# A fused attention and gated-FFN kernel: its front put in another order

## The chip, the core and the metric

The kernel runs on one core of one Trainium2 chip, with one launch. Times are device microseconds of that core; a span is the time from the first to the last instruction of a profiled execution.

## The reference, cut to what matters

```
x: 2048 x 512 float32;  32 heads of 16;  F = 1792
q = x @ wq (32 heads);  k = x @ wk, v = x @ wv (16 wide, one for all heads)
a = softmax(q k^T / 4) v, heads side by side, @ wo
b = ((x @ w_gate) * (x @ w_up)) @ w_down
g = sigmoid(sum(x * gate_w))
out = g * a + (1 - g) * b
```

## The kernel before, in words

**Precision.** Each projection splits both operands into a high part (fp32r) and the rest, low part, and adds three products: high by high, low by high, high by low (`mm3`, `proj`). So a projection of a block of 512 rows of x with 128 output columns is four chunks of 128 inputs times three products: twelve matmuls of 128 by 512.

**Blocks and units.** x is handled in four blocks of 512 rows (c = 0 to 3). Each is transposed on TensorE (`x_trans0` for block 0, tile by tile; `x_trans` for the others, chunk by chunk) and split: `split` makes the high part on ScalarE and the low part on VectorE, both out of PSUM; chunks in `pool` are copied twice by ScalarE and the low part is made by GpSimd. `split2` makes both parts of something that lies in SBUF on GpSimd. K and V of a block come from one projection (`kv`), whose evacuation makes K (called KK, on ScalarE and then VectorE), and `v_trans` turns V. K's and V's weights are split by `kv_split`, the gate's by `gate_split`.

Q is projected in groups of 128 columns (g = 0 to 3, eight heads each), stored to DRAM as two tensors (`dq`, high and low) and fetched back by unit (`q_fetch`, six DMAs a unit): a unit is one tile of 128 query rows of one group. There are 64 units.

**Two passes over the scores.** For each unit, pass one (`p1`) computes scores with queries on the partitions, a matmul of 48 rows by 512 keys, and VectorE takes each row's maximum (L717). When the 32 maxima of a unit are there, `p1_end` reduces them and sends them through DRAM into two rows of the unit's Q tile. Pass two (`p2`) computes the scores transposed, with the maximum subtracted by those rows, and ScalarE takes the exponent (L758). `pv` multiplies by V, two key tiles at a time, eight matmuls in four column groups, and after 16 key tiles the accumulator is evacuated. The score matmuls use half of TensorE's rows (partitions 0 to 63 or 64 to 127), so two can run beside each other; so do the matmuls of the jobs below (L885).

**Jobs.** The rest of the work, projections of Q, the FFN's gate, up and down products and the output projection, is cut into jobs of 12 products, each issued in two halves of 64 rows, one half of the array each, the second half one job behind the first. Jobs fill the places between the scores.

**What sets the order.** Instructions are issued in program order on each engine. Until the lead loop the order is written out by hand (L779 to L811). The lead loop (L953) then interleaves pass one with `LEADJOBS` jobs until 25 steps of pass one (50 maxima) are done. The main loop goes through a written pattern (`ORDER`, `APART`) of pass one, pass two, job halves and PV; model times decide only which job is ready. When it ends, the jobs left over are issued, and then the last unit's output: sums and picks out of the accumulator (L673), a last output projection in two halves of columns (L150, 128 by 256), and the final stores.

**The front, L779 to L811.** Fourteen transposes of the identity; block 0 of x; K/V of block 0; Q of group 0 from block 0, stored whole; the fetch of units 0 and 1; loads of the other Q weights; transposes of blocks 1 and 2; K/V of block 1; then K/V of blocks 2 and 3 and block 3's transposes with five steps of pass one (`steps`) between them. Block 3's first two chunks have their low part made by GpSimd. The loads of x (`load_x`) are all issued at the start on SyncE's queue (SP), but for block 0's last tile and the small weights, which ScalarE issues. A load waits on SP until the one eight places earlier has landed.

Of the kernel before, what the change touches and what calls it, by code (L numbers as in the profile page):

```python
# [26 lines left out]
NG = 4  # L27
NT = 4
# [17 lines left out]
PV_IN, PV_ROUND, PV_LAST, PV_END, PV_OUT = 331.0, 866.0, 438.0, 617.0, 647.0  # L46
NB = 7
LAT, LAT_LAST = 1.0, 0.5
LEADJOBS = 6
O0, O1 = 0, 0  # L50


# [17 lines left out]
def mix_kernel(ctx: ExitStack, tc: tile.TileContext, x, wq, wk, wv, wo, wg, wu, wd, gw, out):  # L70
# [86 lines left out]
    def bank(i, name):  # L157
        return psum.tile([128, 512], F32, name=name, tag=f"bank{i}")
# [4 lines left out]
    def load_x(c):  # L163
        if c < 2:
            xn = [w512("y", F32, 8) for _ in range(NT)]
        else:
            pairs = [work.tile([128, 2, 512], F32, name="P", tag="P", bufs=PBUF) for _ in range(2)]
            xn = [t[:, i] for t in pairs for i in range(2)]
        for t in range(NT):
            eng = nc.scalar if c == 0 and t == NT - 1 else nc.sync  # L170
            eng.dma_start(xn[t], x2[c * 512 + t * 128:c * 512 + t * 128 + 128, :])
        return xn

    def stage(src, tag="wn", bufs=4):
        n = w512(tag, F32, bufs)
        nc.sync.dma_start(n.rearrange("p (k f) -> p k f", k=4) if len(src.shape) == 3 else n, src)
        return n
# [21 lines left out]
                nc.sync.dma_start(xT[c][v][k].bitcast(F32), xd[c][v * 4 + k])  # L199

    dq, dqat = {}, {}

    def at(t, fn):
        later(max(0.0, t - clock["T"]), fn)
# [13 lines left out]
    def q_fetch(u):  # L218
        c, g, t = units[u]
        q = Q[u] = work.tile([128, 4, 128], F32R, name="Q", tag="Q", bufs=QB)  # L220
        for d, rows in zip(dq[c, g], ((0, 32), (16,))):
            for half in range(2):
                for r in rows:
                    b = half * 64 + r
                    src = d[half * 64:half * 64 + 64, t * 128:(t + 1) * 128]
                    nc.sync.dma_start(q[b:b + 16].bitcast(F32), src.rearrange("(s d) q -> d s q", d=DH))
        qat[u] = clock["T"] + 6000.0

    kvn = work.tile([128, 4, 32], F32, name="kvn", tag="oT", bufs=2)
    nc.scalar.dma_start(kvn[:, :, 0:16], wk_v)  # L230
    nc.scalar.dma_start(kvn[:, :, 16:32], wv_v)
    gwn = work.tile([128, 128], F32, name="gwn", tag="rb", bufs=2)
    nc.scalar.dma_start(gwn[0:4], gw.rearrange("(k p) -> k p", p=128))
    xns = {0: load_x(0)}
    wqn = [stage(wq_v[:, :, 0:128])]
    xns[1] = load_x(1)
    xns[2] = load_x(2)
    xns[3] = load_x(3)
# [6 lines left out]
    def kv_split():  # L245
        nc.vector.tensor_copy(kvs2[0], kvn)
# [7 lines left out]
        split2(*wqs[0], wqn[0])  # L254

    def gate_split():

        p = bank(6, "warm")
        nc.tensor.transpose(p[:, 0:4], gwn[0:4], ident[0:4, 0:4])
        hi, lo = (wkvt[:, v].rearrange("p (k c) -> p k c", k=4)[:, :, 58] for v in range(2))  # L260
        split(hi, lo, p[:, 0:4])

    def x_trans0():
        xT[0] = x_tiles()
        hi, lo = xT[0][2:]
        for t in range(NT):
            p = bank(2 + t, "px")
            for k in range(4):
                nc.tensor.transpose(p[:, KS[k]], xns[0][t][:, KS[k]], ident)  # L269
            split(hi[:, :, KS[t]], lo[:, :, KS[t]], p.rearrange("p (k q) -> p k q", k=4))  # L270
            if t == 1:
                kv_split()
                gate_split()

    def x_trans(c, ks=range(4), pool=()):
        xn = xns[c]
        if c not in xT:
            xT[c] = [[w[:, k] for k in range(4)] for w in (woh, wol)] if c == 3 else \
                x_tiles((("hh", "hl"), ("wdh", "wdl"))[c - 1])
        for k in ks:  # L280
            p = bank(2 + (4 * c + k) % 5, "px")
            for t in range(NT):
                nc.tensor.transpose(p[:, KS[t]], xn[t][:, KS[k]], ident)  # L283
            if k in pool:
                xs = w512(("yt", "osb")[k % 2], F32, 2)
                nc.scalar.copy(xT[c][0][k], p)
                nc.scalar.copy(xs, p)
                nc.gpsimd.tensor_tensor(xT[c][1][k], xs, xT[c][0][k].bitcast(F32), op=OP.subtract)
            else:
                split(xT[c][0][k], xT[c][1][k], p)  # L290

    kvs = {}

    def kv(c, between=None):
        p = ms_bank(c % 2)
# [9 lines left out]
        nc.scalar.activation(Kc, p, AF.Identity, bias=kneg)  # L305
        nc.vector.scalar_tensor_tensor(Kc, Kc.bitcast(F32), klow, p, op0=OP.mult, op1=OP.add)  # L306
        nc.scalar.copy(kvs[c], p)

    def v_trans(c):
        pv = bank(7, "pv")  # L310
# [19 lines left out]
    def q_evac(c, g, p, fast=False):  # L330
        qh, ql = w512("oh", F32R, 2), w512("ol", F32R, 2)
        if fast:
            split(qh, ql, p)
# [219 lines left out]

    def ffn_jobs():
        for c in range(NC):
            yield from q_jobs(c, range(c == 0, NG))
        pend = None
        for i, (c, f) in enumerate(order):
            if f == 0:
                hat = {}  # L560
            gu, wdn = {}, []
            yield ffn_job(i, 0, gu, hat, wdn)
            wdn.append(stage(wd[f * 128:(f + 1) * 128, :], "wdn", 2))
            if st["idle"]:
                later(4000.0, lambda wdn=wdn: wd_split(wdn))
            yield ffn_job(i, 1, gu, hat, wdn)
            if f == NF - 1:
                ends = [pend, down_jobs(c, FGS[-1], hat)]
                for k in LAST:
                    yield next(ends[k])  # L570
                pend = None
            elif pend and f != NF - 2:
                yield from pend
                pend = None
            for fs in FGS[:-1]:
                if f == fs[-1]:
                    pend = down_jobs(c, fs, hat)
# [198 lines left out]
            later(0.0, out)  # L776


    p = bank(6, "warm")  # L779
    for i in range(14):  # L780
        nc.tensor.transpose(p[:, KS[i % 4]], ident, ident)  # L781
    x_trans0()
    kv(0)
    p = ms_bank(1)
    mm_all(p, proj(wqs[0], xT[0]))
    q_evac(0, 0, p, True)
    for u in range(2):
        q_fetch(u)
    for g in range(1, NG):
        wqn.append(stage(wq_v[:, :, g * 128:(g + 1) * 128]))  # L790
    x_trans(1)
    x_trans(2)
    kv(1)
    v_trans(0)
    x_trans(3, (0, 1), (0, 1))
    done = 0

    def steps(n, banks):
        nonlocal done
        for i in range(2 * n):  # L800
            p1(done + i // 2, i % 2, banks[i])
        done += n

    steps(1, (3, 7))
    x_trans(3, (2, 3))
    kv(2, lambda: steps(1, (4, 5)))
    steps(1, (6, 2))
    for g in range(1, NG):
        split2(*wqs[g], wqn[g])
    v_trans(1)  # L810
# [204 lines left out]
```

## Time and profile before

| | us |
|---|---|
| median of 3 runs (lowest, highest) | 1617.45 (1617.38, 1618.65) |
| span of the profiled execution | 1616.4 |
| TensorE busy in it | 1608.8 |
| VectorE busy | 1382.5 |
| ScalarE busy | 1227.2 |
| GpSimd busy | 732.9 |
| mean granted TensorE clock | 0.999 |

For the profiled execution the trace gives the span alone, without what lies around it; the runs of the same kernel are 1.0 to 2.2 us longer than that span.

How to read the rows below. A row of the timeline has start, duration, engine, line of the kernel, operation, output and inputs, shape, how many equal instructions follow each other, and in brackets the engine's idle time ahead of it and what ended that. A row of windows has the stretch and its length, then the busy time (and instructions) of PE, the weight loads, DVE, ACT and POOL, the granted clock, the DMA engines' share and GB/s. A row of groups has the count, busy time in us, mean ns of one, and the idle time ahead of them. PE is TensorE, PEld its weight loads, DVE VectorE, ACT ScalarE, POOL GpSimd, SPq SyncE's queue. Matmuls overlap, so one that takes 0.39 us can follow its neighbour by 0.23.

### The profile page before, as it was taken

The numbers are of one execution on the slowest core, as the hardware profiler recorded it, in microseconds if no ns is written. First come the engines' busy times: TensorE is split into PE (matmuls) and PEld (weight loads), VectorE is DVE, ScalarE is ACT, GpSimd is POOL, SyncE is SP. The second block draws the span as 40 slices with busy tenths as digits, with TensorE's granted clock in tenths as the row PEclk, the third lists the DMA queues.
The fourth block names the chain that finished last, engine by engine and source line by source line (L and its number), as shares of the span: only waits on it lengthen the run. The fifth ranks groups of instructions, "written<-read, shape, count | busy, mean of one in ns | idle before, by whom it ended". The sixth has DMA issues, their size and how long they took to land.

```text
span 1616.4 us, 35356 instructions
## 1 busy us (share of the span) xinstructions
PE 1608.8 (100%) x13139; PEld 1029.4 (64%) x13139; DVE 1382.5 (86%) x2412; ACT 1227.2 (76%) x2368; POOL 732.9 (45%) x869
## 2 busy tenths in 40 slices
PE   9999999999999999999999999999999999999998
PEld 7766666666666666666666666666666666666564
DVE  6988888888888888888888888888888888888870
ACT  4477777777778777777788787787788787787786
POOL 3325652634644542535543651642643642643633
PEclk9999999999999999999999999999999999999999
DMA  4463321212322221212231221222231221221111
GB/s 155 147 238 114 95 71 54 65 54 69 94 68 71 67 74 52 66 48 72 64 102 59 74 66 53 67 59 61 66 112 48 72 79 49 65 66 56 41 30 40
DMA packets 185255, 121.45 MB, mean 75 GB/s; under 512 B 46328, under 2 KB 154748, under 8 KB 185084
## 3 DMA queue, kind: packets, MB, share of 16 engines
q1 hardware_dynamic: 183732, 118.74, 24.3%
q8 instruction: 103, 1.69, 0.4%
q10 hardware_dynamic: 1352, 0.46, 0.1%
q14 instruction: 68, 0.56, 0.1%
HBM read 82.96 MB, written 36.17 MB: 74 GB/s over the span
## 4 chain that ended last, share of the span: by engine, by line
PE 99%; ACT 1%; DVE 0%; issue 0%; POOL 0%; DVEq 0%; POOLq 0%; ACTq 0%
PE ms L885 34%; PE acc L770 29%; PE s L757 18%; PE s L716 15%; PE ms L150 1%; ACT P L758 1%; PE px L283 0%; PE warm L781 0%; PE wo L150 0%; ACT yt L354 0%; PE pv L312 0%; ACT osb L774 0%; PE px L269 0%; POOL P L251 0%; DVE KK L306 0%
## 5 line engine op out<-in xcount | busy, mean ns | idle before, releaser
L717 DVE TENSOR_REDUCE mx<-s 128x1 f32<-128x512 f32 x2048 | 1308.8, 685 | 168.9 <-PE s L716 82.6
L758 ACT ACTIVATE P<-s 128x512 f32<-128x512 f32 x2048 | 1079.3, 606 | 260.1 <-PE s L757 221.4
L757 PE MATMUL s<-Q,KK 50*128 50x512 f32 x2048 | 746.0, 411 | 0.1
L716 PE MATMUL s<-KK,Q 48*128 48x512 f32 x2048 | 691.5, 406 | 0.7 <-ACT gb L315 0.5
L770 PE MATMUL acc<-P,V 128*32 128x512 f32 x4096 | 493.5, 598 | 0.0
L757 PEld LDWEIGHTS s<-Q,KK 50*128 50x128 f32 x2048 | 352.2, 185 | 177.7 <-issue 94.7
L716 PEld LDWEIGHTS s<-KK,Q 48*128 48x128 f32 x2048 | 337.9, 185 | 109.2 <-ACT P L758 48.5
L885 PE MATMUL ms<-xh,wh 64*128 64x512 f32 x920 | 338.4, 391 | 0.0
L885 PE MATMUL ms<-xl,wh 64*128 64x512 f32 x920 | 337.3, 391 | 0.0
L885 PE MATMUL ms<-xh,wl 64*128 64x512 f32 x920 | 321.5, 391 | 0.0
L770 PEld LDWEIGHTS acc<-P,V 128*32 128x32 f32 x4096 | 108.5, 109 | 236.3 <-issue 196.1
L528 POOL TENSOR_TENSOR hf<-gs 128x512 f32<-128x512 f32 x56 | 71.9, 1284 | 355.9 <-ACT gs L519 340.6
L355 POOL TENSOR_TENSOR y<-y,yt 128x512 f32<-128x512 f32 x79 | 101.3, 1286 | 230.4 <-ACT yt L354 223.4
L885 PEld LDWEIGHTS ms<-xl,wh 64*128 64x128 f32 x920 | 164.5, 186 | 10.2
L885 PEld LDWEIGHTS ms<-xh,wh 64*128 64x128 f32 x920 | 163.5, 186 | 10.3 <-POOL wl L138 0.4
L885 PE MATMUL ms<-wdh,hh 64*128 64x512 f32 x448 | 165.0, 393 | 0.0
L885 PE MATMUL ms<-wdl,hh 64*128 64x512 f32 x448 | 165.0, 391 | 0.0
L885 PEld LDWEIGHTS ms<-xh,wl 64*128 64x128 f32 x920 | 157.1, 186 | 10.1 <-issue 0.3
L885 PE MATMUL ms<-wdh,hl 64*128 64x512 f32 x448 | 158.7, 391 | 0.0
L138 POOL TENSOR_TENSOR wl<-wn,wh 128x512 fp32r<-128x512 f32 x117 | 150.5, 1287 | 9.4
L774 ACT COPY osb<-acc 128x512 f32<-128x512 f32 x64 | 37.5, 586 | 76.0 <-PE acc L770 76.0
L629 POOL TENSOR_TENSOR oT<-raw,rb 128x128 f32<-128x128 f32 x63 | 29.0, 461 | 126.0 <-DMA rb<-dr 126.0
(156 smaller groups left out, 1314.4 us busy)
## 6 DMA issues: line engine op xcount, KB each, us to landing
do<-osb SPq DMA_DIRECT2D x63, 256.0 KB
wn<-in_B_w_gate_dram SPq DMA_DIRECT2D x56, 256.0 KB
wn<-in_B_w_up_dram SPq DMA_DIRECT2D x56, 256.0 KB
wdn<-in_B_w_down_dram SPq DMA_DIRECT2D x56, 256.0 KB
Q<-dq SPq DMA_DIRECT2D x384, 32.0 KB
raw<-do SPq DMA_DIRECT2D x252, 32.0 KB
dq<-oh SPq DMA_DIRECT2D x16, 256.0 KB
dq<-ol SPq DMA_DIRECT2D x16, 256.0 KB
```

The lines of the kernel that those rows point to most:

```text
L138: nc.gpsimd.tensor_tensor(lo, src, hi.bitcast(F32), op=OP.subtract)
L150: nc.tensor.matmul(p, l, r, start=start and i == 0, stop=stop and i == len(prods) - 1)
L355: nc.gpsimd.tensor_tensor(y[c, t], y[c, t], tmp, op=OP.add)
L528: nc.gpsimd.tensor_tensor(hf, gu[0], gu[1], op=OP.mult)
L629: nc.gpsimd.tensor_tensor(dst, raw[:, 0], rb, op=OP.mult)
L716: nc.tensor.matmul(p, q[r, slot], KK[r, kq * 512:(kq + 1) * 512], start=True, stop=True)
L717: nc.vector.tensor_reduce(mx[u][:, half * 4 + slot, kq:kq + 1], p, axis=AX.X, op=OP.max)
L757: nc.tensor.matmul(p, KK[r, j * 128:(j + 1) * 128], q[r].rearrange("p s q -> p (s q)"), start=True, stop=True)
L758: nc.scalar.activation(P[s][:, half], p, AF.Exp, scale=0.25)
L770: nc.tensor.matmul(acc[u][b:b + 32, :], V[:, j + i], src[:, half], start=(j == 0), stop=(j == NJ - 2))
L774: nc.scalar.copy(osb, acc.pop(u))
L885: nc.tensor.matmul(p, lhs[HALVES[l]], rhs[HALVES[l]], start=(i == 0 and (l == 0 or j.apart)), stop=(end and (l == 1 or j.apart)))
```

## The change

The order of the front is written anew. Block 0's four x tiles are loaded two on SP and two on ScalarE's queue, ahead of everything else, with wq's first group behind them; K/V's weights come later, and block 3 of x is loaded behind the first fetch of Q. Three more identity transposes stand behind each of block 0's last three tiles. Q of group 0 is projected first, in two halves of 256 columns with stores of their own (`q_first`), and unit 0 is fetched after the first half is stored; K/V's weights are split behind that. Blocks 2 and 3 of x have all their low parts made by GpSimd out of ScalarE's copies. Twelve steps of pass one, not five, stand in the front, in groups of two steps (four matmuls) between the K/V blocks. Q of group 1 from block 0 is projected in the front as well (at full height, twelve matmuls), and the lead loop takes four jobs instead of six: with Q of group 1 that makes five early jobs.

```diff
-LEADJOBS = 6
+LEADJOBS = 4
@@ load_x
-            eng = nc.scalar if c == 0 and t == NT - 1 else nc.sync
+            eng = nc.scalar if c == 0 and t % 2 else nc.sync
@@ q_fetch
-        for d, rows in zip(dq[c, g], ((0, 32), (16,))):
+        parts = dq[c, g]
+        if len(parts) > 2:
+            parts, t = parts[t // 2 * 2:t // 2 * 2 + 2], t % 2
+        for d, rows in zip(parts, ((0, 32), (16,))):
@@ loads
+    xns = {0: load_x(0)}
+    wqn = [stage(wq_v[:, :, 0:128])]
     kvn = work.tile([128, 4, 32], F32, name="kvn", tag="oT", bufs=2)
...
-    xns = {0: load_x(0)}
-    wqn = [stage(wq_v[:, :, 0:128])]
     xns[1] = load_x(1)
     xns[2] = load_x(2)
-    xns[3] = load_x(3)
@@ x_trans0
-            if t == 1:
-                kv_split()
-                gate_split()
+            if t:
+                warm(3)
-    def x_trans(c, ks=range(4), pool=()):
+    def x_trans(c, ks=range(4), banks=(), pool=()):
...
-        for k in ks:
-            p = bank(2 + (4 * c + k) % 5, "px")
+        for k, b in zip(ks, banks):
+            p = bank(b, "px")
@@
+    def q_first():
+        qh, ql = w512("oh", F32R, 2), w512("ol", F32R, 2)
+        dq[0, 0], stores = [], []
+        for i, cols in enumerate(HALF):
+            p = ms_bank(i)[:, 0:256]
+            mm_all(p, [(l, r[:, cols]) for l, r in proj(wqs[0], xT[0])])
+            split(qh[:, cols], ql[:, cols], p)
+            for src in (qh, ql):
+                d = dram.tile([128, 256], F32, name=f"dq{len(stores)}", bufs=1)
+                dq[0, 0].append(d)
+                stores.append(lambda d=d, src=src, cols=cols: nc.sync.dma_start(d, src[:, cols].bitcast(F32)))
+        dqat[0, 0] = 0.0
+        return stores
+
+    def q_evac(c, g, p, now=False):
+        qh, ql = w512("oh", F32R, 2), w512("ol", F32R, 2)
+        if now:
+            qs = w512("gs", F32, 3)
+            nc.scalar.copy(qs, p)
+            split2(qh, ql, qs)
             q_store(c, g, qh, ql)
@@ ffn_jobs
-            yield from q_jobs(c, range(c == 0, NG))
+            yield from q_jobs(c, range(2 * (c == 0), NG))
@@ the front
-    kv(0)
-    p = ms_bank(1)
-    mm_all(p, proj(wqs[0], xT[0]))
-    q_evac(0, 0, p, True)
-    for u in range(2):
-        q_fetch(u)
+    split2(*wqs[0], wqn[0])
+    stores = q_first()
+    kv_split()
+    gate_split()
+    for f in stores[:2]:
+        f()
+    q_fetch(0)
+    x_trans(1, banks=(2, 3, 4, 5))
+    kv(0, 0)
+    x_trans(2, banks=(1, 2, 3, 4), pool=range(4))
+    xns[3] = load_x(3)
     for g in range(1, NG):
         wqn.append(stage(wq_v[:, :, g * 128:(g + 1) * 128]))
-    x_trans(1)
-    x_trans(2)
-    kv(1)
-    v_trans(0)
-    x_trans(3, (0, 1), (0, 1))
+    for f in stores[2:]:
+        f()
+    q_fetch(1)
...
-            p1(done + i // 2, i % 2, banks[i])
+            p1(done + i // 2, i % 2, (5, 6, 7, 0)[(2 * done + i) % 4])
...
-    steps(1, (3, 7))
-    x_trans(3, (2, 3))
-    kv(2, lambda: steps(1, (4, 5)))
-    steps(1, (6, 2))
-    for g in range(1, NG):
+    steps(2)
+    kv(1, 1, lambda: steps(2))
+    split2(*wqs[1], wqn[1])
+    v_trans(0, 2)
+    x_trans(3, (0, 1), (3, 4), range(4))
+    steps(2)
+    x_trans(3, (2, 3), (1, 2), range(4))
+    steps(2)
+    kv(2, 3)
+    q1 = proj(wqs[1], xT[0])
+    p = ms_bank(4)
+    mm_all(p, q1[:6], True, False)
+    steps(2)
+    mm_all(p, q1[6:], False, True)
+    q_evac(0, 1, p, True)
+    st["q"] += 1
+    for g in range(2, NG):
         split2(*wqs[g], wqn[g])
-    v_trans(1)
-    kv(3, lambda: steps(2, (3,4,5,6)))
+    v_trans(1, 2)
+    kv(3, 1, lambda: steps(2))
```

More of the change, by code (lines that the diff above doesn't have):

```diff
@@ L201, in mix_kernel @@
     dq, dqat = {}, {}
+    HALF = (slice(0, 256), slice(256, 512))
     def at(t, fn):
@@ L253, in kv_split @@
             eng.tensor_copy(w[:, :, :, 50:58], kvs2[v][:, :, 16:32].rearrange("p k (h d) -> p k h d", h=2))
-        split2(*wqs[0], wqn[0])
     def gate_split():
@@ L292, in mix_kernel, with kv @@
     kvs = {}
-    def kv(c, between=None):
-        p = ms_bank(c % 2)
+    def kv(c, b, between=None):
+        p = ms_bank(b)
         prods = proj((wkvh, wkvl), xT[c])
@@ L307, in kv, with v_trans @@
         nc.scalar.copy(kvs[c], p)
-    def v_trans(c):
-        pv = bank(7, "pv")
+    def v_trans(c, b=7):
+        pv = bank(b, "pv")
         for t in range(4):
@@ L328, in gates @@
         nc.vector.tensor_scalar(gb, gg, -1.0, 1.0, op0=OP.mult, op1=OP.add)
-    def q_evac(c, g, p, fast=False):
+    def q_first():
         qh, ql = w512("oh", F32R, 2), w512("ol", F32R, 2)
-        if fast:
-            split(qh, ql, p)
+        dq[0, 0], stores = [], []
[15 more added lines that the diff above has]
+            split2(qh, ql, qs)
             q_store(c, g, qh, ql)
@@ L776, in pv, with warm, steps @@
             later(0.0, out)
-    p = bank(6, "warm")
-    for i in range(14):
-        nc.tensor.transpose(p[:, KS[i % 4]], ident, ident)
-    x_trans0()
-    kv(0)
-    p = ms_bank(1)
-    mm_all(p, proj(wqs[0], xT[0]))
-    q_evac(0, 0, p, True)
-    for u in range(2):
-        q_fetch(u)
+    wp = bank(6, "warm")
+    def warm(n):
+        for i in range(n):
+            nc.tensor.transpose(wp[:, KS[i % 4]], ident, ident)
+    warm(14)
+    x_trans0()
+    split2(*wqs[0], wqn[0])
[9 more added lines that the diff above has]
+    xns[3] = load_x(3)
     for g in range(1, NG):
         wqn.append(stage(wq_v[:, :, g * 128:(g + 1) * 128]))
-    x_trans(1)
-    x_trans(2)
-    kv(1)
-    v_trans(0)
-    x_trans(3, (0, 1), (0, 1))
+    for f in stores[2:]:
+        f()
+    q_fetch(1)
     done = 0
-    def steps(n, banks):
+    def steps(n):
         nonlocal done
         for i in range(2 * n):
-            p1(done + i // 2, i % 2, banks[i])
+            p1(done + i // 2, i % 2, (5, 6, 7, 0)[(2 * done + i) % 4])
         done += n
-    steps(1, (3, 7))
-    x_trans(3, (2, 3))
-    kv(2, lambda: steps(1, (4, 5)))
-    steps(1, (6, 2))
-    for g in range(1, NG):
+    steps(2)
[15 more added lines that the diff above has]
+    for g in range(2, NG):
         split2(*wqs[g], wqn[g])
-    v_trans(1)
-    kv(3, lambda: steps(2, (3,4,5,6)))
+    v_trans(1, 2)
+    kv(3, 1, lambda: steps(2))
     xT_first = dict(xT)
```

## The prediction

> **What bounds the kernel now.** I read the page first: busy time per engine and the chain that ended last.
>
> ```profile
> PE 1608.8 (100%) x13139; PEld 1029.4 (64%) x13139; DVE 1382.5 (86%) x2412; ACT 1227.2 (76%) x2368; POOL 732.9 (45%) x869
> PE 99%; ACT 1%; DVE 0%; issue 0%; POOL 0%; DVEq 0%; POOLq 0%; ACTq 0%
> ```
>
> TensorE (PE) holds 99% of the chain, so the sum of its work is fixed and an edit can only remove or add time in which it waits, at the two ends. The instruction order says the same: from the first to the last score in the main loop both programs issue the same kinds of matmul in the same order, only that every job sits one place later. So I read the timeline of the front, and then of the end.
>
> ```profile
> 24.58 0.69 DVE L717 TENSOR_REDUCE mx<-s 128x1 f32<-128x512 f32 x1
> L717 DVE TENSOR_REDUCE mx<-s 128x1 f32<-128x512 f32 x49 | 30.1, 680 | 1.3 <-PE s L716 1.1
> 34.55:60.50 25.95, 25.95 (x180) 20.73 (x180) 24.99 (x47) 3.96 (x8) 7.60 (x8) 1.00 0.21 74
> 60.50 0.50 PE L757 MATMUL s<-Q,KK 50*128 50x512 f32 x1
> 71.24 1.92 PE L770 MATMUL acc<-P,V 128*32 128x512 f32 x16
> ```
>
> The first maximum is reduced at 24.58 us, the first exponent score is issued at 60.50, the first PV at 71.24. The second row groups VectorE (DVE) from 24 to 61 us: 49 maxima, 30.1 us (0.614 each), with only 1.3 us of waiting ahead of them. The third (span, then PE, weight loads, DVE) has DVE at 24.99 of 25.95 us. So **DVE bounds the front from the first maximum to the first exponent score**: 50 maxima lie between them, before and after the change alike.
>
> **The change, part by part.**
>
> *First Q projection ahead of K/V.* On PE, the opening of the program, before (ms is a projection's bank, xh/xl the transposed x, P the K/V weights, wh/wl the Q weights):
>
> ```order
> L269 MATMUL px<-ident,y 128x128 x8
> L150 MATMUL ms_200<-xh,P 128x512 x8
> L150 MATMUL ms_200<-xl,P 128x512 x4
> L150 MATMUL ms_217<-xh,wh 128x512
> L283 MATMUL px<-ident,y 128x128 x16
> L283 MATMUL px<-ident,P 128x128 x16
> L150 MATMUL ms_330<-hh,P 128x512 x2
> ```
>
> And after, from the end of the Q projection to the first maxima (s):
>
> ```order
> L150 MATMUL ms_210<-xl,wh 128x256
> L261 MATMUL warm<-ident,gwn 128x4
> L284 MATMUL px<-ident,y 128x128 x16
> L150 MATMUL ms_284<-xh,P 128x512 x8
> L150 MATMUL ms_284<-xl,P 128x512 x4
> L284 MATMUL px<-ident,P 128x128 x16
> L733 MATMUL s_367<-KK,Q 128x512
> L733 MATMUL s_376<-KK,Q 128x512
> L150 MATMUL ms_379<-hh,P 128x512 x2
> ```
>
> Q (ms_193 and ms_210, two halves of 256 columns) now precedes K/V (ms_284), and the first maxima stand ahead of the second K/V block instead of behind it and a third set of transposes.
>
> ```profile
> 7.50 0.66 PE L269 MATMUL px<-ident,y 128*128 128x128 f32 x4 [0.70 <-DMA y<-in_A_x_dram]
> 8.82 0.61 POOL L137 CAST wh<-wn 128x512 fp32r<-128x512 f32 x1
> 9.52 1.27 POOL L138 TENSOR_TENSOR wl<-wn,wh 128x512 fp32r<-128x512 f32 x1
> 1610.06 0.28 PE L150 MATMUL wo<-woh,ol 128*128 128x256 f32 x1
> 1610.17 0.28 PE L150 MATMUL wo<-wol,oh 128*128 128x256 f32 x1
> 16.05 1.91 PE L283 MATMUL px<-ident,y 128*128 128x128 f32 x16
> 16.86 0.33 SPq L210 DMA_DIRECT2D dq<-oh  x1
> 18.94 5.95 SPq L226 DMA_DIRECT2D Q<-dq  x12
> 6.08 4.43 SPq L171 DMA_DIRECT2D P<-in_A_x_dram  x8
> ```
>
> The last x tile came at 7.50 us; in the new order of loads the weights follow close behind it, so I put wn at 6.7. GpSimd (POOL) then needs 0.61 + 1.27 us: wl at 8.65. 24 half-width matmuls at 0.115 (two neighbours in the tail) end at 11.4, against 16.05. Half 0 is evacuated and stored from 10.8; a store took 2.08 us to let the fetch go (16.86 to 18.94), a fetch 0.5 us to issue (5.95/12), so the six for unit 0 are out by 15.8 and land, with another 2, by 17.8. SP has x2's loads ahead of the store; x2's and x3's were all issued by 10.5 before, and x3's four now follow the fetch.
>
> K/V of block 0 must wait for its weights, which DVE now splits behind Q's evacuation (ends 12.6).
>
> ```profile
> 7.32 0.22 DVE L246 CAST rb<-kvn 128x128 fp32r<-128x128 f32 x1
> 8.37 0.15 DVE L143 TENSOR_TENSOR P<-warm,P 128x4 fp32r<-128x4 f32 x1
> 15.14 0.39 PE L150 MATMUL ms<-xl,wh 128*128 128x512 f32 x1
> 15.37 0.39 PE L150 MATMUL ms<-xh,wh 128*128 128x512 f32 x1
> 22.85 0.69 ACT L305 ACTIVATE KK<-ms,kneg 128x512 fp32r<-128x512 f32 x1 [2.10 <-PE ms L150]
> 23.57 0.75 DVE L306 SCALAR_TENSOR_TENSOR KK<-KK,klow,ms 128x512 fp32r<-128x512 f32 x1 [1.23 <-ACT KK L305]
> ```
>
> The split ran from 7.32 to 8.52, so it is done at 13.8 (block 1's transposes cover it on PE); twelve matmuls 0.23 apart end at 16.5; ScalarE (ACT) and DVE make K by 0.69 + 0.75: 18.3. Sixteen transposes (1.91) fill PE until 18.5. **First maxima matmul 18.5, first reduce 19.05: 5.5 us earlier.** Q has 0.7 us to spare there.
>
> *Chunks split on ACT and POOL.* The low halves of x2 and of x3's second half leave DVE.
>
> ```profile
> L143 DVE TENSOR_TENSOR wol<-px,woh 128x512 fp32r<-128x512 f32 x2 | 1.3, 685 | 1.2 <-ACT woh L142 1.2
> 25.36 0.62 ACT L287 COPY yt<-px 128x512 f32<-128x512 f32 x1
> 25.84 0.63 ACT L286 CAST woh<-px 128x512 fp32r<-128x512 f32 x1
> 26.06 1.29 POOL L288 TENSOR_TENSOR wol<-yt,woh 128x512 fp32r<-128x512 f32 x1 [15.27 <-ACT yt L287]
> ```
>
> Inside the bound stretch that frees 1.3 us of DVE (x2's four lay ahead of it). In return ACT makes two passes per chunk, 0.48 apart, eight for a block: 18.9 to 22.8 for x2, which lets the second K/V block start only at 20.0 (its bank is a transpose's). POOL's eight halves at 1.29 and the split of wq1 (0.61 + 1.27) run from 20 to 32.3, each ahead of its reader.
>
> *Maxima woven in.* Four maxima matmuls use four banks and the next four wait for their reduces, while PE, in order, keeps whole K/V blocks between them. Stepping through the order with the durations above, DVE stands idle at 21.5 (0.4, bank), 25.4 (0.4, K block 1), 30.7 to 32.4 and 33.2 to 33.7 (2.2: sixteen maxima are used up and K block 2, twelve matmuls behind the sixteenth, must come first), 36.3 (1.3, second half of Q 1), 40.9 (0.8, K block 3 and wl of Q 2) and some 0.3 more: 5.3 us, against 1.3 before. PE enters the lead loop at 39.0 instead of 34.55, but with 24 maxima done instead of 10.
>
> Each such group changes PE's tile shape twice.
>
> ```profile
> 32.00 0.40 PE L150 MATMUL ms<-wol,P 128*128 128x512 f32 x1
> 32.33 0.30 PEld L716 LDWEIGHTS s<-KK,Q 48*128 48x128 f32 x4 [0.36 <-issue]
> 32.99 0.30 PEld L150 LDWEIGHTS ms<-woh,P 128*128 128x128 f32 x2 [0.37 <-issue]
> ```
>
> Four maxima matmuls, two by two, are worth 0.46 us and held PE from 32.23 to 32.99: 0.3 more. The stations above contain this for each group; two of the groups lie on the way to K blocks 2 and 3. [...]
>
> So the first exponent score moves by −5.5 (start) − 1.3 (DVE's work) + 4.0 (more idling) = **−2.8 us**, to 57.7. Its other condition is the maxima's way through DRAM.
>
> ```profile
> 51.86 0.22 DVE L731 TENSOR_REDUCE mt<-mt 128x32 fp32r<-128x64 f32 x1
> 52.11 1.34 SPq L737 DMA_DIRECT2D dm<-mt  x4
> 57.13 0.78 SPq L744 DMA_DIRECT2D Q<-dm  x2
> ```
>
> Unit 0's maxima end at 49.3 (52.08 before). Behind the store SP has one pair of Q stores, which wait for POOL's split of the first lead job (53.1), then the fetch: 54.2, landed 56.4, 1.3 us ahead of need.
>
> *Five early jobs.* Before the first PV 132 job matmuls instead of 180: 48 less, of which 24 are Q 1, done in the front at full height. So one job is left over, and since the loop is the same it comes out at the very end. On PE, before, from the last PV on:
>
> ```order
> L770 MATMUL acc<-P,V 32x512 x8
> L673 MATMUL sums<-osb,sel_24094 32x128 x4
> L673 MATMUL pick<-osb,sel_24093 32x128 x4
> L150 MATMUL wo<-woh,oh 128x256
> L150 MATMUL wo<-woh,ol 128x256
> ```
>
> And after:
>
> ```order
> L787 MATMUL acc<-P,V 32x512 x8
> L921 MATMUL ms_25510<-wdl,hh 128x512
> L921 MATMUL ms_25510<-wdh,hh 128x512
> L921 MATMUL ms_25510<-wdh,hl 128x512
> ...
> L921 MATMUL ms_25594<-wol,oh 128x512
> L690 MATMUL sums<-osb,sel_24201 32x128 x4
> ```
>
> Nineteen matmuls of two jobs (seven and twelve, all on one 64-row half, so no two run beside each other) now stand between the last PV and the sums.
>
> ```profile
> 1598.15 0.39 PE L885 MATMUL ms<-woh,ol 64*128 64x512 f32 x1
> 1598.38 0.39 PE L885 MATMUL ms<-wol,oh 64*128 64x512 f32 x1
> 1606.28 2.30 PE L770 MATMUL acc<-P,V 128*32 128x512 f32 x16
> 1609.26 0.43 PE L673 MATMUL sums<-osb,sel 128*32 128x128 f32 x8 [0.69 <-ACT osb L774]
> ```
>
> On one half they follow at 0.23: 19 × 0.23 = 4.4 us from the end of PV (1608.4 to 1608.6), where PE idled 0.7 to 0.9 for the copy of the accumulator. **The sums and all behind them come 3.5 us later.** The two evacuations and their additions lie beside this tail.
>
> **Sum:** −2.8 + 3.5 = +0.7, on the profiled span of 1616.4: 1617.1. The median of the runs, 1617.45, lies 1.05 above that span, so **1618.1 us**: no change. (About 0.2%, 3.2 us, is what a measurement of this kernel can tell from no change: below 1614.2, above 1620.7.)
>
> **Rivals.**
>
> *The weaving keeps DVE full* (the rows for: only 1.3 us idle in the old front). If it idles no more than before, the exponent scores come 6.8 us earlier; with the tail −3.3: 1614.1; with no idling at all, −4.6: 1612.9. I take 1613.5. Against it: with four banks the thirteenth to sixteenth maxima cannot outlast twelve matmuls, K and 0.5 us of latency.
>
> *The clock drops in the front.* The windows give the granted clock third from the end.
>
> ```profile
> 6.00:8.00 2.00, 1.30 (x10) 0.96 (x9) 1.85 (x6) 1.32 (x4) 0.07 (x1) 1.00 1.07 374
> 8.00:10.00 2.00, 1.28 (x5) 0.96 (x4) 1.72 (x6) 0.58 (x1) 1.91 (x5) 0.77 1.04 381
> 10.00:12.00 2.00, 2.00 (x6) 1.54 (x6) 0.00 (x0) 0.00 (x0) 0.79 (x1) 0.50 1.06 391
> ```
>
> PE was busy two thirds of 6 to 10 us, and the clock fell to 0.50 for the stretch behind. The nine added warm transposes fill most of that, and my sum has full speed; but PE still waits for wl, and at half speed from 9.1 to 12.5 the 24 Q matmuls end 1.8 us later: 1619.9. [...]
>
> *Slower: the maxima's fetch is caught on SP.* It stands behind the Q stores that wait for POOL, and POOL is fuller (q1, wq2 and wq3 ahead of the first lead job's split). With two such splits (1.9 us each) late, the fetch is 3.8 us later, 1.3 of it free: the scores wait 2.5 to 3 and the time is 1620.9. It decides once that split ends after 54.4 us. For it: SP is in order. Against: POOL was busy 7.60 of 25.95 us in the lead.
>
> **How the numbers follow.** Forecast 0.50; DVE full 0.15; clock 0.17; SP 0.18. Faster by over 0.2% is the first rival, 0.15; slower by as much the third, 0.18; within it the forecast and the clock, 0.67. The unknown prices (arrival of wn and Q, idling in the weave) are worth some 1.5 us either way; 1613.4 to 1621.6 takes in all cases but their ends.
>
> **What would show it.** The first maximum near 19, the first exponent score near 57.7, the first PV near 68.4; DVE idle around 31 us; clock 1.00 from 8 to 12; sums 4.4 us behind the last PV. I am wrong if the first exponent score comes before 55 or after 60, or if the nineteen matmuls find room ahead of the last PV.

## The result, and the profile after

The changed kernel takes **1627.81 us** (median of 4 runs, 1627.62 to 1628.21) against 1617.41 us before (median of 4 runs, 1616.85 to 1618.65): a ratio of 1.0065, 95% interval 1.005 to 1.0079. It is 10.4 us slower, and outside the forecast range of 1613.4 to 1621.6.

The profiled execution has a span of 1625.8 us, 9.4 us more than the one of before. First the busy times and the chain, from the page of the changed kernel, and its group of maxima matmuls.

```profile
PE 1614.2 (99%) x13148; PEld 1036.7 (64%) x13148; DVE 1379.1 (85%) x2407; ACT 1230.4 (76%) x2375; POOL 741.5 (46%) x875
PE 96%; POOL 1%; DVE 1%; ACT 1%; issue 0%; DMA 0%; SPq 0%; DVEq 0%; POOLq 0%
L733 PE MATMUL s<-KK,Q 48*128 48x512 f32 x2048 | 689.5, 406 | 5.2 <-ACT yt L371 4.3
```

TensorE still carries nearly the whole chain, but its share fell from 99% to 96%, and one wait stands out: 4.3 us for a yt copy on ScalarE. I then laid the starts of the 256 PV groups of the two programs (sixteen PV matmuls each, four groups to a unit) beside each other; they say where the two drift apart. These are the rows of the first PV, and of the last one with the sums behind it, in the timeline of TensorE (start, duration).

```profile
68.86 1.92 PE L787 MATMUL acc<-P,V 128*32 128x512 f32 x16
...
1612.21 1.92 PE L787 MATMUL acc<-P,V 128*32 128x512 f32 x16
1618.60 0.42 PE L690 MATMUL sums<-osb,sel 128*32 128x128 f32 x8
```

| PV (number, start before, start after) | after − before | step |
|---|---|---|
| 0: 71.24, 68.86 | −2.38 | front −2.4 |
| 196: 1255.69, 1254.20 | −1.49 | +0.9 over 1186 us |
| 198: 1265.62, 1270.72 | +5.10 | **+6.6 in 17 us** |
| 255 (last): 1606.28, 1612.21 | +5.93 | +0.8 |
| end of the span: 1616.4, 1625.8 | +9.4 | tail +3.5 |

The front and the tail came out within half a microsecond of the forecast. What sank it stands in a place where I had put nothing: between 1254 and 1271 us. Here are the 5 us windows of the changed kernel (stretch; its length; busy time of PE, weight loads, DVE, ACT, POOL; granted clock third from the end), and the timeline behind them.

```profile
1250.00:1255.00 5.00, 5.00 (x43) 4.01 (x43) 4.63 (x10) 5.00 (x11) 4.69 (x5) 1.00 0.22 62
1255.00:1260.00 5.00, 1.79 (x16) 0.43 (x8) 2.21 (x5) 0.19 (x1) 4.84 (x6) 0.90 0.10 26
1260.00:1265.00 5.00, 3.87 (x18) 0.88 (x18) 0.69 (x1) 2.64 (x5) 3.43 (x5) 0.50 0.28 82
1265.00:1270.00 5.00, 5.00 (x42) 4.04 (x40) 3.71 (x6) 3.86 (x8) 1.14 (x1) 0.92 0.00 0
```

```profile
1250.08 1.29 POOL L545 TENSOR_TENSOR hf<-gs 128x512 f32<-128x512 f32 x1 [5.83 <-ACT gs L536]
1250.51 0.69 ACT L371 ACTIVATE yt<-ms,gb 128x512 f32<-128x512 f32 x1
1253.01 0.72 ACT L371 ACTIVATE yt<-ms,gg 128x512 f32<-128x512 f32 x1
...
1257.88 1.26 POOL L138 TENSOR_TENSOR wl<-wn,wh 128x512 fp32r<-128x512 f32 x1
1259.10 3.83 POOL L372 TENSOR_TENSOR y<-y,yt 128x512 f32<-128x512 f32 x3
1260.39 0.69 ACT L371 ACTIVATE yt<-ms,gb 128x512 f32<-128x512 f32 x1 [5.21 <-POOL y L372]
1261.13 0.79 PE L733 MATMUL s<-KK,Q 48*128 48x512 f32 x1 [4.34 <-ACT yt L371]
```

Read it from the top. A yt copy takes a finished product out of its accumulator bank, scaled, on ScalarE; GpSimd then adds it to a block of the output, y (`y_add`). There are two yt buffers. GpSimd begins a burst of nine products and splits at 1250.08 (hf, its two halves, wd, two weights), 9 us without a gap. Meanwhile ScalarE makes two scaled copies of y blocks, at 1250.51 and 1253.01, and so takes both yt buffers. Their additions are GpSimd's work, and stand behind the burst: 1259.10. A third copy needs a buffer, so ScalarE, in order, stops for 5.21 us (the row at 1260.39). The exponentials behind it stop too, and TensorE stops for 4.34 us. Scores and products take turns in the same seven banks (`claim`), and TensorE's next score matmul starts at 1261.13, 0.05 us after the third copy has emptied its bank and before the first of the exponentials behind that copy, begun at 1260.98 and some 0.6 long, has ended: the bank of this product is what it waited for. Then the clock: it fell to 0.50 during the wait and is there when TensorE starts again. In the kernel before, one copy alone falls into the same burst, the row below, and in the whole program none waited over 0.7 us for a buffer.

```profile
1256.07 0.69 ACT L354 ACTIVATE yt<-ms,gg 128x512 f32<-128x512 f32 x1
```

### The profile page after: what moved, and what is told of

Read it like the earlier page. It is cut to its first block, busy times and chain, and to the rows that moved or that the text cites. A ratio compares the mean times of both kernels' runs of the same rounds, so it can differ in the third digit from the quotient of the medians.

```text
span 1625.8 us, 35376 instructions
## 1 busy us (share of the span) xinstructions
PE 1614.2 (99%) x13148; PEld 1036.7 (64%) x13148; DVE 1379.1 (85%) x2407; ACT 1230.4 (76%) x2375; POOL 741.5 (46%) x875
## 4 chain that ended last, share of the span: by engine, by line
PE 96%; POOL 1%; DVE 1%; ACT 1%; issue 0%; DMA 0%; SPq 0%; DVEq 0%; POOLq 0%
PE ms L921 33%; PE acc L787 29%; PE s L774 18%; PE s L733 14%; PE ms L150 1%; DVE mx L734 1%; DMA wn<-in_A_wq_dram 0%; POOL wl L138 0%; ACT P L775 0%; PE wo L150 0%; ACT yt L371 0%; POOL ol L138 0%; POOL y L372 0%; POOL wh L137 0%; DMA rb<-dr 0%
```

## The experiments

Theory A: with one job less ahead of the loop, each job meets other neighbours. At one place, where block 2's last down projections and an output projection fall behind the first product of block 3, three y copies fall into one GpSimd burst, and two yt buffers are too few. Theory B: the new front does it, by what it leaves on queues. Theory C: the clock falls there by itself. Each comparison gives the ratio to the kernel before, run beside it (medians 1616.67 to 1617.14). Early jobs are counted here up to the first PV: seven in the kernel before, with LEADJOBS at 6, and six in the changed one, Q of group 1 being one of them. (The description of the change, which counts the lead loop's own, has one less.)

### Is it the new front, or the number of jobs?

The changed kernel with seven early jobs, as before had, and the kernel before with six:

```diff
-LEADJOBS = 4
+LEADJOBS = 5
```

```diff
-LEADJOBS = 6
+LEADJOBS = 5
```

> The changed kernel with one early job more (LEADJOBS 5), so that seven jobs are done before the main loop, as in the kernel before, and every job sits at its old place; the new front stays. Theory A (the shift of the job stream by one place lines three y evacuations up with one GpSimd burst around 1255 us, about 8 us, and leaves nineteen matmuls for the tail, 3.5 us): the stop at 1255 us is gone, the tail is the one of before, and one job's 2.8 us of TensorE go back ahead of the first PV: 1616 to 1619 us. Theory B (the new front itself does it, through what it leaves behind on queues and buffers, whatever the number of jobs): 1624 to 1628. Theory C (the clock falls at that time by itself): 1624 to 1628 with the low clock at the same time of the span.

> The kernel before with one early job less (LEADJOBS 5 instead of 6): six jobs before the main loop, as in the changed kernel, with the old front untouched. Theory A: the stop near 1255 us appears here as well (7 to 8 us) and the tail is 3.5 us longer, less at most 2.8 us in front: 1624 to 1629. Theory B: no stop, 1616 to 1621. Theory C: 1616 to 1621 unless the drop falls by chance.

The new front with seven jobs took 1621.76 us (1.0033, 1.002 to 1.0045); its span behind the last PV is 10.1 us, as in before, and no yt copy waits over 1 us. The old front with six took **1629.94 us** (1.0077, 1.0064 to 1.009), and in its timeline stands the same stop:

```profile
1263.97 0.69 ACT L354 ACTIVATE yt<-ms,gb 128x512 f32<-128x512 f32 x1 [5.13 <-POOL y L355]
1264.71 0.56 PE L716 MATMUL s<-KK,Q 48*128 48x512 f32 x1 [4.27 <-ACT yt L354]
```

The stop goes with the number of jobs, in both fronts: B and C fall. That the first of the two came in above its 1616 to 1619 is a matter of the front; it is taken up below. The second is 0.9 above its 1624 to 1629; in its profiled execution the clock was also at 0.50 from 8.9 to 12.3 and from 60.1 to 66.9 us, ahead of the first PV.

### Is it the two yt buffers?

The copies of the output projections go to the two osb buffers, which otherwise take the accumulator of PV, once for each of the 64 units. No instruction changes its place.

```diff
-    def y_add(c, t, p, gcol, n=1):
+    def y_add(c, t, p, gcol, n=1, tag="yt"):
...
-            tmp = w512("yt", F32, 2)
+            tmp = w512(tag, F32, 2)
...
-   lambda p, i: y_add(c, t, p, gg[...]), ...
+   lambda p, i: y_add(c, t, p, gg[...], tag="osb"), ...
```

In the changed kernel, as a control in the one before, and in the one before with six early jobs:

> The changed kernel with its instructions in the same order on every engine, but the scaled copies of the output projections (sixteen of the y evacuations) go to the osb buffers instead of the yt buffers, so that a third y copy in a GpSimd burst needs no yt buffer that waits for an addition. Theory A: the two yt buffers are what binds, the stop at 1255 to 1270 us goes with its slow clock, 7 to 8 us: 1619 to 1621, the tail still 3.5 us late. Theory B: the burst or the front does it, 1626 to 1628. Theory C: 1626 to 1628 with the clock low at 1260 us though no engine waits before it.

> Control: the same change of buffers in the kernel before, which shows no stop there. All theories: 1617.4, within 1.5 us. If it is faster by more than that, other copies also wait for yt buffers in the kernel before, and the run before it is no clean yardstick for the gain of the buffers alone.

> The kernel before with one early job less (1629.9 us, with the stop near 1260 us) and the output projections' copies in the osb buffers. Theory A: the stop and its slow clock go here as they went in the changed kernel, 6.5 to 7.5 us: 1622.5 to 1623.5, and the tail stays 3.5 us longer than before's. Rival (in this front the osb copy waits for something else, or the burst itself is the bound): 1628 to 1630.

| kernel | with yt | with osb | ratio of the second to before |
|---|---|---|---|
| changed | 1627.81 | **1620.90** | 1.0023 (1.0014 to 1.0032) |
| before | 1617.02 | 1617.49 | 1.0002 (0.9994 to 1.0011) |
| before, six early jobs | 1629.94 | 1622.22 | 1.0031 (1.002 to 1.0041) |

6.9 and 7.7 us are gained where there was a stop, and nothing where there was none. Of the 7.7, by the two profiled executions, 6.1 lie at the stop (from PV 192 to 198 the old front with six jobs loses 6.8 us against before with yt, 0.6 with osb). Another 1.7 lie ahead of the first PV (73.00 and 71.28 us): there the clock stayed at 0.50 for 6.8 us behind 60.1 in the first and for 3.4 in the second, a stretch that the change of buffers does not touch. In the first of the three kernels the same place now reads:

```profile
1252.82 0.72 ACT L371 ACTIVATE osb<-ms,gg 128x512 f32<-128x512 f32 x1
...
1254.82 0.76 ACT L371 ACTIVATE yt<-ms,gb 128x512 f32<-128x512 f32 x1
```

```profile
1255.00:1260.00 5.00, 5.00 (x46) 2.10 (x40) 3.47 (x7) 3.49 (x7) 4.84 (x6) 1.00 0.07 16
1260.00:1265.00 5.00, 5.00 (x46) 3.15 (x46) 4.84 (x8) 4.89 (x10) 4.92 (x7) 1.00 0.31 92
```

The burst is as long as it was (POOL 4.84 of 5 us), the third copy comes at 1254.82, with no wait, and TensorE is full at full clock. So it is not the burst by its load, but its place ahead of the additions together with the number of buffers.

### How the price grows with the wait

The other way to free the buffers is to let the additions go first. At this one place (the first product of block 3, number 42) the weight splits that end the burst are given to GpSimd later: both of them, or only the second. Nothing else moves on any engine.

```diff
-                ffn_split(n + 2)
+                if n == 42:
+                    later(6000.0, lambda: ffn_split(n + 2))
+                else:
+                    ffn_split(n + 2)
```

> The changed kernel (1627.8 us) with one thing moved on GpSimd alone, at the one place: the three y additions stand ahead of the two weight splits (3.8 us) of the burst at 1250 us instead of behind them. Buffers, TensorE's, ScalarE's and VectorE's orders are the same. Theory A: the first addition ends at 1256.6 instead of 1260.4, the third copy follows at once, TensorE waits 0.6 us instead of 4.3 and its clock stays up: 6.3 to 7.1 us less, 1620.7 to 1621.5. [...]

For the second, the first weight's split stays where it was:

```diff
+                    ns, landed = staged.pop(n + 2)
+                    one = w_split(ns[0], ("wh", "wl"), WB, landed)
+                    def rest():
+                        W[n + 2] = [one, w_split(ns[1], ("wh", "wl"), WB, landed)]
+                        at(W[n + 2][1][1] + 300.0, lambda: ffn_stage(n + 4))
+                    later(6000.0, rest)
```

> The same, half way: the three y additions stand between the two weight splits. The first addition ends near 1258.5, so TensorE should wait 2.4 us instead of 4.3. If the stop's price is the wait alone: 1623.0 to 1623.6. If the clock falls as well, as it did within 2.2 us of the start of the wait in the changed kernel, and stays at half for some 5 us of work behind it: 1625 to 1626.2.

They took **1620.96 us** (1.0027, 1.0016 to 1.0038) and **1624.33 us** (1.0047, 1.0033 to 1.006). The first lies in its range. The second lies between its two: the clock fell, but for less than the 5 us of work that the upper range had taken. The restart of TensorE in the one and in the other, and for the second the clock around it:

```profile
1257.14 0.50 PE L736 MATMUL s<-KK,Q 48*128 48x512 f32 x1 [0.57 <-ACT yt L371]
```

```profile
1258.50 0.49 PE L742 MATMUL s<-KK,Q 48*128 48x512 f32 x1 [2.44 <-ACT yt L371]
```

```profile
1259.00:1260.00 1.00, 1.00 (x13) 0.40 (x16) 0.69 (x1) 1.00 (x3) 1.00 (x2) 0.92 0.74 218
1260.00:1261.00 1.00, 1.00 (x11) 0.01 (x1) 0.00 (x0) 0.40 (x1) 0.92 (x3) 0.50 0.00 0
...
1263.00:1264.00 1.00, 1.00 (x10) 0.78 (x10) 0.62 (x2) 1.00 (x3) 0.00 (x0) 0.88 0.43 120
```

| TensorE waits | clock at 0.50 | wait + half of the busy time at 0.50 | step from PV 192 to 198 |
|---|---|---|---|
| none (osb) | no | 0 | +0.3 |
| 0.57 | no | 0.6 | +1.1 |
| 2.44 | 3.4 us | 2.4 + 1.7 = 4.1 | +4.6 |
| 4.27 (old front, six jobs) | 3.4 us | 4.3 + 1.7 = 6.0 | +6.8 |
| 4.34 (changed kernel) | 6.8 us, 4.7 of them busy | 4.3 + 2.4 = 6.7 | +7.1 |

Take off the last column what the loop drifts there anyway (0.3; 0.6 in the old front, with osb), and the two agree within 0.2 us. About a third of the stop's price is the clock, not the wait. The same wait was followed by 3.4 us of slow clock in one front and by 6.8 in the other; the windows of the old front, where it fell at 1265.0 and was back at 1268.4:

```profile
1265.00:1266.00 1.00, 1.00 (x6) 0.20 (x8) 0.69 (x1) 1.00 (x4) 1.00 (x2) 0.50 0.18 52
1268.00:1269.00 1.00, 1.00 (x8) 0.33 (x6) 0.00 (x0) 0.00 (x0) 0.00 (x0) 0.79 0.00 0
```

In one of the five executions of the kernel with the 2.44 us wait, at 1622.64 us, the mean granted clock was 1.000 and not 0.998 or 0.999, and it was 1.7 us faster than the median, which is what the slow clock costs by the third column (that execution has no trace of its own).

### Does any shift of the jobs do this?

Five early jobs in the changed kernel:

```diff
-LEADJOBS = 4
+LEADJOBS = 3
```

> The changed kernel with one early job less still (LEADJOBS 3, five jobs before the main loop), yt buffers as they were. Theory A says that the stop depends on where the job stream falls against the GpSimd bursts, not on its being late as such: this place may have a stop, none, or several; each costs about 7 us. Without one: the front saves up to 2.8 us (or less, VectorE being the bound), the tail holds one job more (2.8 to 5.5 us): 1621 to 1624; with one: 1628 to 1631. If the stop came from lateness in itself it would be here for certain, and longer than 5.2 us of ScalarE's waiting.

1624.81 us (1.005, 1.0038 to 1.0063), 0.8 above the range without a stop. The longest wait of a yt copy for an addition is 0.7 us: no stop. The tail is 16.2 us from the last PV on (13.6 with six early jobs, 10.1 with seven), and the front loses time to VectorE and then to the clock: ahead of the first exponent scores VectorE is full and TensorE is not, and behind that the clock is at 0.50 for 3.4 us.

```profile
55.00:58.76 3.76, 2.55 (x10) 0.97 (x9) 3.76 (x8) 0.66 (x2) 1.89 (x2) 1.00 0.33 105
58.76:62.17 3.41, 3.41 (x16) 2.73 (x18) 2.80 (x5) 1.68 (x3) 0.00 (x0) 0.50 0.32 121
```

So of five, six and seven early jobs only six meets the burst: a matter of place, not of lateness.

### What in the front carries it

Three parts, each undone in the changed kernel with osb (1620.90 us), and one done alone in the kernel before.

The weaving undone (the first `steps(2)` stays):

```diff
-    kv(1, 1, lambda: steps(2))
+    kv(1, 1)
...
     x_trans(3, (0, 1), (3, 4), range(4))
-    steps(2)
     x_trans(3, (2, 3), (1, 2), range(4))
-    steps(2)
...
     mm_all(p, q1[:6], True, False)
-    steps(2)
...
-    kv(3, 1, lambda: steps(2))
+    kv(3, 1)
```

> The changed kernel with the osb buffers for the output projections' copies (1620.9 us, no stop at 1255 us), and only the first of its six groups of four maxima woven into the front; the other twenty are left to the lead loop, whose jobs, and the main loop, are the same. Theory D (VectorE bounds the front, so maxima must start early): the lead loop begins some 6 us sooner, near 34 us, but with 46 maxima ahead at 0.61 us, so the first exponent score comes at 63 to 64 instead of 58.0: 1625.5 to 1627.5 us. Rival P (TensorE in its order bounds the front, and five groups cost it two changes of tile shape of 0.3 us each and buy nothing): the first exponent score at 56 to 58: 1619 to 1621.

The chunks back on VectorE:

```diff
-    x_trans(2, banks=(1, 2, 3, 4), pool=range(4))
+    x_trans(2, banks=(1, 2, 3, 4))
...
-    x_trans(3, (2, 3), (1, 2), range(4))
+    x_trans(3, (2, 3), (1, 2))
```

> The same base (1620.9 us), with the low halves of x2 and of x3's second half back on VectorE instead of ScalarE and GpSimd. Theory D: two subtractions, 1.3 us, come back into VectorE's bound stretch, and x2's four (2.7 us) ahead of the first maxima of K block 0 hold up the first reduces by 1 to 2 us, while ScalarE's second pass goes; 0.5 to 2.5 us slower: 1621.4 to 1623.4. Rival P: TensorE's order sets the front, K block 1 is ready sooner since its bank waits for fewer copies: 0 to 1.5 us faster, 1619.4 to 1620.9.

Without the warm transposes:

```diff
-            if t:
-                warm(3)
```

> The same base (1620.9 us) without the nine warm transposes between x0's. Theory W (the front's gain against the profiled execution of before, 2.4 us at the first PV, is for the most part a clock that stays up, since a kernel with the old front and a steady clock had its first PV at 69.4 us): without them TensorE is idle more between 6 and 10 us, the granted clock falls to 0.50 for 2 to 4 us near 9 us and the first PV moves from 68.7 to 70 to 71: 1622 to 1623.5. Rival (the new order itself holds the clock, or the waits hide it): 1620.5 to 1621.

The chunks alone, in the kernel before:

```diff
-    x_trans(2)
+    x_trans(2, pool=range(4))
...
-    x_trans(3, (2, 3))
+    x_trans(3, (2, 3), (2, 3))
```

> One part of the change alone, in the kernel before: the low halves of x2's four chunks and of x3's second half are made by ScalarE's second pass and GpSimd instead of VectorE. Theory D (VectorE bounds the front): six subtractions, 3.9 us of VectorE, leave it, of which 1.3 to 2 us lie behind the first maximum; undone in the new front the same edit cost 3.8 us: 1614 to 1616. Rival P: TensorE's order and the bank that ScalarE's second pass holds set the old front, whose maxima start late anyway: 1616.5 to 1618.5.

The five results:

| | median | ratio to before | first exponent score |
|---|---|---|---|
| base, changed with osb | 1620.90 | 1.0023 (1.0014 to 1.0032) | 57.98 |
| no weaving | 1631.63 | 1.0098 (1.0084 to 1.0112) | 65.75 |
| chunks on VectorE | 1624.66 | 1.005 (1.0036 to 1.0063) | 62.32 |
| no warm transposes | 1620.84 | 1.0024 (1.0014 to 1.0033) | 58.17 |
| before, chunks moved | 1617.56 | 1.0003 (0.9994 to 1.0012) | 58.88 |

Without the weaving VectorE stands mostly idle from 24 to 40 us (busy 3.85 of 16), TensorE then waits for it, and its clock falls besides, to 0.50 from 57.8 to 71.4 us: 10.7 us, where I had expected 4.6 to 6.6. How much of it the clock holds was not measured apart. Windows of that kernel:

```profile
24.00:40.00 16.00, 14.19 (x73) 10.76 (x72) 3.85 (x8) 8.05 (x17) 13.87 (x14) 1.00 0.26 83
56.00:60.00 4.00, 2.84 (x7) 1.09 (x6) 3.86 (x10) 0.00 (x0) 1.66 (x2) 0.72 0.36 134
57.76:71.41 13.65, 12.40 (x36) 7.05 (x38) 12.34 (x24) 2.88 (x5) 0.00 (x0) 0.50 0.29 99
```

The chunks are worth 3.8 us in the new order, more than the 2.5 I had allowed: with the chunks back on VectorE x2's four low halves (2.48 us of VectorE, in a row from 19.85) stand ahead of the first reduce, which comes at 22.25 instead of 19.24, and TensorE waits for the reduces behind them, as two rows of that kernel's timeline show. Behind these waits its clock is at 0.50 for 3.4 us, the third row, a window, so up to 1.7 of the 3.8 is the clock.

```profile
19.85 2.48 DVE L143 TENSOR_TENSOR wdl<-px,wdh 128x512 fp32r<-128x512 f32 x4 [1.14 <-ACT wdh L142]
22.98 2.51 PE L733 MATMUL s<-KK,Q 48*128 48x512 f32 x4 [0.76 <-DVE mx L734]
24.89:28.30 3.41, 3.41 (x8) 2.29 (x9) 2.23 (x4) 0.00 (x0) 1.32 (x2) 0.50 0.26 76
```

In the old front the same edit is worth nothing, because there TensorE itself is full; its windows with the edit show it:

```profile
24.00:40.00 16.00, 16.00 (x82) 11.13 (x82) 12.39 (x22) 6.18 (x13) 10.55 (x10) 1.00 0.19 53
40.00:58.88 18.88, 18.88 (x145) 15.52 (x143) 18.30 (x35) 2.52 (x5) 7.63 (x8) 1.00 0.29 102
```

The warm transposes do nothing that can be measured. Theory W failed: without them the clock held as well (1.000 over each of the nine executions), though TensorE was busy only 1.03 of the 2 us from 8 to 10.

```profile
8.00:10.00 2.00, 1.03 (x8) 0.84 (x8) 1.47 (x3) 0.42 (x1) 1.10 (x1) 1.00 1.02 375
```

## Why the prediction was wrong, point by point

**"Since the loop is the same" — the step that failed.** I compared the order on TensorE alone, found the same kinds of matmul with every job one place later, and set the loop's cost at nothing. The jobs' evacuations run on ScalarE and GpSimd, beside other neighbours than before. At one place of 1600 us that costs 6.6 to 7.1 us, by the chain of waits that the runs showed link by link: burst ahead of additions, two yt buffers, ScalarE in order, the bank of the waiting product, TensorE, clock. With the buffers or the order at that place mended, 6.9 us return. None of my rivals was this one; all of the 0.18 that I gave to a slower kernel lay in the front.

It could have been looked for in the order of GpSimd, which I did not go through for the loop. Its instructions around that place, after the change (and not before it, nor with seven early jobs; the old front with six has the same):

```
TENSOR_TENSOR hf<-gs 128x512
CAST hh<-hf 128x512
TENSOR_TENSOR hl<-hf,hh 128x512
CAST wdh<-wdn 128x512
TENSOR_TENSOR wdl<-wdn,wdh 128x512
CAST wh<-wn 128x512
TENSOR_TENSOR wl<-wn,wh 128x512
CAST wh<-wn 128x512
TENSOR_TENSOR wl<-wn,wh 128x512
TENSOR_TENSOR y<-y,yt 128x512 x3
```

Three additions in a row behind nine instructions (9.0 us in the trace), with two buffers to wait in. The order alone does not settle it, though. At 829 us the changed kernel has three additions in a row behind eleven instructions (9.6 us), and no copy waits there, because only one of the three, at 824.41, falls due during that burst. The times of the copies have to be laid beside the order.

**The tail, +3.5: right.** From the last PV to the end of the span it was 10.1 us and is 13.6; from the last PV to the sums 2.98 (1606.28 to 1609.26) and now 6.39. The nineteen half-height matmuls run there at 0.23.

**The front, −2.8 at the first exponent score: the number was right, the reason half right.** It came at 58.12 (−2.4), the first PV 2.4 sooner. But the control above has before's front, instruction for instruction, and there:

```profile
22.70 0.69 DVE L717 TENSOR_REDUCE mx<-s 128x1 f32<-128x512 f32 x1
58.64 0.49 PE L757 MATMUL s<-Q,KK 50*128 50x512 f32 x1
69.37 1.06 PE L770 MATMUL acc<-P,V 128*32 128x512 f32 x8
```

The execution of before that I worked from had lost 1.9 us to a low clock between 9 and 12.5 us; this one did not. Of 21 runs of before beside the first set, two had a span over 1616 us and the others 1614.7 to 1615.6. Against a usual execution the first reduce came 3.3 us earlier (19.36 against 22.70), not the 5.5 of the sum, and what lies between it and the first exponent score grew by 2.8, as the sum had it (−1.3 + 4.0). So the new front is 0.5 us ahead at the first PV, and it has 24 matmuls (2.8 us) less to do by then. With equal work, seven jobs each, it is behind: first PV at 74.02 against 69.37. These are the windows of the new front with seven jobs:

```profile
56.00:60.00 4.00, 3.02 (x23) 2.21 (x19) 3.97 (x8) 0.59 (x1) 1.52 (x2) 1.00 0.51 177
64.00:68.00 4.00, 3.26 (x27) 2.62 (x29) 2.72 (x7) 3.14 (x7) 1.84 (x2) 1.00 0.36 134
```

TensorE idles 0.98 and 0.74 us there, and its first exponent score comes at 62.81. From 8 us to the first PV, in this kernel and in the control:

```profile
8.00:74.02 66.02, 62.33 (x395) 47.13 (x393) 49.60 (x94) 28.96 (x60) 28.91 (x30) 1.00 0.36 122
8.00:69.37 61.37, 60.14 (x386) 46.64 (x386) 51.43 (x92) 25.41 (x51) 22.20 (x25) 1.00 0.38 130
```

TensorE idles 3.7 us in the first and 1.2 in the second, so 2.5 of the 4.65 us are holes. For the other 2.2 it was busy; how much of that is the changes of tile shape is not shown.

**"VectorE bounds the front": only in the new order.** The row that I had quoted for the old lead loop has VectorE at 24.99 of 25.95 us and TensorE at 25.95 of 25.95. I took the second for a sum that nothing could change, though it is the fuller of the two. Moving VectorE's work away gained nothing in the old front. In the new one, where TensorE has holes, VectorE's idle time is what counts, as the weaving and chunk runs show. From the first reduce to the first exponent score VectorE stood idle for 6.4 us (busy 32.37 of 38.76); the sum had 5.3, where its own pieces add to 5.4. The sum set that against 1.3 before, but 1.3 is the wait ahead of the maxima alone: the old front's idle time over the same stretch was 3.3 us (busy 32.62 of 35.92). The two main groups of the new front, with the wait just ahead of the first of each:

```profile
L734 DVE TENSOR_REDUCE mx<-s 128x1 f32<-128x512 f32 x48 | 29.5, 681 | 5.0 <-PE s L733 5.0
L307 DVE SCALAR_TENSOR_TENSOR KK<-KK,klow,ms 128x512 fp32r<-128x512 f32 x3 | 2.2, 747 | 2.0 <-ACT KK L306 1.9
```

**The rivals.** The clock held at 1.00 from 8 to 12 us, and did so without the transposes too. The maxima's fetch was not caught: the store left at 50.33, the fetch at 54.19, where I had put 54.2.

```profile
50.33 1.30 SPq L754 DMA_DIRECT2D dm<-mt  x4
54.19 0.56 SPq L761 DMA_DIRECT2D Q<-dm  x2
```

**The sum as it came**, against a usual run of before (1617.0): stop +6.9, tail +3.5, front and loop together about +0.4. That is 10.8 us. No version tried here beats the kernel before: the new front with the stop mended is 3.9 us slower, and the tail of the missing job is nearly all of that.

## What to carry to other kernels

An edit that shifts a stream of jobs by one place has to be followed on every engine that evacuates them: look for the places where more results fall due than there are buffers, while the engine that empties them is in a long run of other work, and go by the times as well as by the order. Where a profile of one execution is the base of a sum, see whether it has a low clock that most executions have not, and where a row shows two engines full, neither can be called the bound alone. A wait of TensorE is to be priced with the slow clock that may follow it: here it followed waits of 2.44 and 4.3 us, and not one of 0.57.

## What the runs showed of the hardware

Where the low clock was read in the traces, but for the last few us of a program, it lasted 3.4 us, or 6.8 or 13.65. By the 1 us windows of the changed kernel it fell at 1259.02 (0.51 in the window from 1259) and was back at 1265.84 (0.58 in the window from 1265): 6.8 us, twice that length.

```profile
1258.00:1259.00 1.00, 0.00 (x0) 0.00 (x0) 0.00 (x0) 0.00 (x0) 1.00 (x1) 1.00 0.03 8
1259.00:1260.00 1.00, 0.00 (x0) 0.00 (x0) 0.00 (x0) 0.00 (x0) 1.00 (x2) 0.51 0.42 116
...
1265.00:1266.00 1.00, 1.00 (x8) 0.53 (x6) 0.00 (x0) 0.00 (x0) 0.00 (x0) 0.58 0.00 0
```

With the 2.44 us wait the windows shown above give 1259.84 to 1263.24: 3.4 us, beginning 1.3 us after TensorE had started again. Without the weaving it was low from 57.8 to 71.4 us (the windows shown above), four times that length. In the front of before, the 0.77 from 8 to 10 and the 0.88 of this row give 9.08 to 12.48, again 3.4:

```profile
12.00:14.00 2.00, 2.00 (x10) 1.60 (x9) 0.00 (x0) 0.50 (x1) 0.00 (x0) 0.88 1.06 387
```

The front of before lost the clock in this execution and kept it in that of the control with osb: there it was at 1.00 from 8 to 12 us, with TensorE busy for 1.40 of the 2 us from 8 to 10, against 1.28 here. TensorE was not idle all the time ahead of the falls: in the 3.4 us before them it was busy 1.2 us (changed kernel), 1.3 (2.44 us wait) and 2.0 (front of before), and even 3.06 in the kernel without the weaving:

```profile
54.35:57.76 3.41, 3.06 (x13) 1.33 (x9) 3.38 (x7) 0.58 (x1) 1.88 (x2) 1.00 0.37 138
```

So TensorE's busy time as the profile counts it does not tell when the clock falls: it fell behind 3.06 of 3.41 us busy, and held at 1.03 of 2 without the warm transposes. What makes it fall, and what sets how long it stays low, was not shown.
